# Loading A's first 1024 tokens as pairs, and issuing the first weight columns from ScalarE, in a two-headed attention and state-space kernel

## The chip, the cores and the metric

The kernel runs on one core of one Trainium2 chip. The metric is the time of one execution in device microseconds. A profiled execution also has a span, from its first to its last instruction, which leaves out what lies around it.

## What is computed

Two independent heads read two inputs of 2048 tokens by 448 and write the two halves of one output of 2048 by 896, all in bfloat16.

```python
qkv = (x @ wqkv)                      # A: 16 heads of 28, window of 8, dilation 2
idx = pos[:, None] - off[None, :]     # off = 0, 2, ..., 14
logits = einsum("bhsd,bhswd->bhsw", q, k[idx]) * 28 ** -0.5   # masked where idx < 0
a = einsum("bhsw,bhswd->bhsd", softmax(logits), v[idx]) @ wo
Bu = x2 @ B_bar.T                     # B: diagonal complex state-space model
h[t] = Lam_bar * h[t - 1] + Bu[t]
b = 2 * (h @ C.T).real + x2 * Dskip
out = concatenate([a, b], -1)
```

## The kernel before, in words

**Loads.** SP issues nearly all loads (lines 137 to 171), in the order in which they are written. The weights `wq` of A have 448 rows: three pieces of 128 rows and one of 64. `qk_load` (132) loads a range of the q and of the k columns with one DMA each for the 128-row pieces (134), and a third for the 64 rows (135). It is called for the first 128 columns and then for the other 320. POOL copies the 64 rows to partitions 64 to 127 (214 and 215), since the two halves of a pair of half-row products read them from there. A DMA that is the ninth in a row waits for the first of those before it, as there are eight semaphores for loads. ScalarE issues three small loads (`raw`, 127), the parameters of B.

**Tokens of A.** Tokens 0 to 1023 are loaded with 896-byte packets, one token each: partition p of block t holds token 128 t + p. TensorE transposes them (`XI` 273 for tokens 0 to 511, `XA` 302 and `XH` 317 for 512 to 1023), and `xi`, `xa` and `xh` copy the result into `xT`, channels on partitions and tokens along the row. Tokens 1024 to 2047 are transposed by DMA (164).

**Products of A.** `QS` (342) and `QK` (334) make q and k, 128 channels by 512 tokens at a time; `QK(u, m, 0)` is the full-row part of block m for half u of the tokens, and `QK(u, m, 1)` a pair of 64-row products which TensorE does side by side. `qk` (351) and `qh` (356) copy them from PSUM to `qf`, `kf`, `qh_t` and `kh`. `V_` (485) makes v, even and odd tokens apart. `P` (369) multiplies q with two shifted k at a time on VectorE, `E_` (381) sums over a head's channels on TensorE. Softmax follows (`lt`, `TR`, `sma`, `smb`, `smc`), then the band is laid out through DRAM (`AL`, `ad`, `sp`), and `AV` and `W_` give A's output.

**B.** `BT` is transposed by DMA (`BD` 650), `xt` (673) transposes B's tokens by DMA, `BU`, `BR`, `UP` and the scan (`sa`, `sb`, `sd`) make the states, `DN`, `H_`, `ha` to `kb` complete them, and `C(j, ct)` (826) with `c` (834) gives B's output, which `oc` stores.

**Order.** Nothing is scheduled by a compiler. `ORDER` (32) is one list of steps, found by a planner and written into the file; the loop at 885 executes it, and each engine works through its own instructions in that order. `@37` behind a step names the PSUM banks that it takes, a `.` at the end of a copy puts it on ScalarE, a `=` on VectorE. A step that is late holds all that is behind it on its engine.

Of the kernel before, what the change touches and what calls it, by code (L numbers as in the profile page):

```python
# [29 lines left out]


ORDER = """
WU@0 BD XI0@12 PP@3 xi00. pcopy pa xi30. pb pd_ XI1@4 xi31. xi01. xi21= pc xi20= tf3 QS00@5 ts03 QS10@6 XA10@7 pe
XH1@1 XA11@3 pf qk000. tf4 xa11. ts13 ts23 xa10= xh1= QK050@04 qk010= tf0 P000 ts04 QK021@27 QK031@51 pg QK051 qk051.
qk050. QK041@36 QK040 qk040. QK030 QK020 P040 ts14 ts24 qk031. QS11@4 V_011@03 qk020= QK061@12 P001 rb0 qk021. qk030.
V_111@75 qk041. QK060 ts00 qh000. qh011. V_010 v010. v011. tf5 qk011. P041 P021 tz V_110 v111. qh001. V_100@60 P020
qh010. ts10 QS01@3 qk001. V_001@45 V_101 ts20 rb1 ts05 E_00@1 E_02 ts15 v110. hc0 E_04 V_000 v001. QK100@23 v100. tf1
ts01 QK161@75 v000. P010 P011 ts11 QK101 qk101. v101. P060 QK160 P030 qh101. qk100. qh100. QK130@64 qh110. QK110@30
xt1 P050 E_01@2 QK111 qh111. P051 QK131 ts21 P031 qk110. P061 E_03 E_05 ts25 pk E_06 xt0 P100 QK141@75 xt2 qk111. P111
lt00 lt01 qk131. qk130. QK121@30 QK120 P110 hc1 qk120. xt3 qk121. tf2 V_410@12 V_411 v410= v411. QK151@46 V_511@30  # L40
V_510 v510. v511. QK150 TR0@2 P120 qk150. QK140 qk141. qk140. P101 P130 V_500@13 E_10@0 P121 qk151. ts02 tf6 E_12
V_401@45 LC V_501 v500. v501. tr0= ts06 V_400 P131 E_11@7 E_13 v400. sma0 BU201@62 P151 P150 v401. XR smb0 BU301@13
BU401@45 BU300 P140 BU400 OZ z30. BR31 BU200 z40. BU000@14 P161 z31. ci0. ci2. CD2 E_15 ts12 P141 ci3. z20. P160 E_14
E_16 lt11 lt10 ci1. CD0 CD3 BU001 z00. BU311@36 tx BU310 TR1@7 BR21 BR01 BR41 tr1. BR32 z41. z32. CD1 smc0 AL0@0 z01.
al0. ad0 OP BU210@17 xd0 BR33 z33. sma1 z21. smb1 BU010@53 BU011 xd2 ca6 BU211 BU101@40 BU100 rb2 rb3 BR02 z10. z02.
BR22 z22. ca3 cs6 BU500@24 BR11 smc1 BU501 BU111@51 BU110 pm0 z11. cs3 pm3 BR12 z12. BR23 BR03 z03= AL1@0 al1= z50.
UP3 wo BR13 AL2@5 z23. sp0 UP2 y3. BR51 UP0 z13. UP1 xd3 y2. y1. BU410@20 BU411 z51. ad1 y0= pm4 sa0 al2. BU611@67 ad2
BU601@13 BU511@45 ca4 BR42 sb0 sd0 ts22 BU600 pm2 BU510 z42. z60. BR52 z52. BR43 BR61 pm1 sa2 z43. AL3@2 al3. DN1@1
dn1 BR53 z61. z53. BU610 cs4 DN0@4 dn0 UP4 UP5 BR62 H_21@2 y4= h21 ca1 cs1 H_11@3 y5. H_20@1 sp1 sb2 z62. sd2 AV030@4
ts16 AV011@0 h20 AV010@5 av010. AV001@2 av001. av011. AV000@6 ad3 AV020@5 av000. AV031@2 sp2 av031. xd1 AV021@0 av021.  # L50
H_10@6 BR63 sp3 av020. W_31@2 h11 DN2@0 z63. W_01@1 h10 dn2 av030. W_21@5 w31. W_10@4 ow31 ca2 W_11@2 sa4 H_12@3
W_30@6 UP6 w10. w21. ca0 h12 w30. ow30 H_22@0 w11. ow11 H_01@4 DN3@5 y6. W_20@3 w20. AV131@6 av131. ts26 ow21 AV130@2
av130. ow10 AV101@7 av101. w01. AV100@3 av100. sb4 ow20 ow01 AV120@6 AV110@2 av120. AV121@7 sd4 cs2 sa6 dn3 sb6 sd6
AV111@1 av110. av121. W_70@3 w70. H_00@5 h00 W_50@6 DN4@2 h01 dn4 DN6@7 dn6 av111. DN5@3 dn5 ha24 sw6 W_40@5 ca5
H_02@1 w40. h02 W_71@4 w71. cs0 H_03@2 h03 ow40 cs5 W_61@7 H_13@3 ha16 ow71 ha25 hb16 ow70 W_60@5 ka06 sw4 hb24 W_00@4
h22 W_51@1 ha15 C33@2 w60. w00. c33 W_41@5 C31@4 ow60 sw5 w50. w61. ha14 hb15 w41. h13 C30@6 w51. C32@7 hb14 oc33 c32
oc32 H_23@5 ha26 hb26 h23 hb25 C12@0 ow41 C11@1 kb06 ow51 ka05 kb05 C10@2 ow00 ka04 C20@3 c20 c10 oc10 C22@7 C23@5
C13@3 c30 oc30 oc20 c11 C21@2 ow61 c22 oc22 c12 kb04 oc11 C01@6 c23 ow50 oc23 oc12 c21 C02@1 c01 oc01 c31 oc21 c02 c13
C00@7 c00 oc02 oc31 C03@0 c03 oc00 oc13 oc03
"""  # L60

@with_exitstack
def kernel(
# [49 lines left out]
    def evict(e, o, i):  # L113
        (ACT.copy if e == "A" else V.tensor_copy)(o, i)  # L114
# [8 lines left out]
    wq_r = A_wqkv[0:384].rearrange("(f p) n -> p f n", p=128)

    raw = const.tile([G, 3, 2, 64], BF16, tag="raw")
    for i, vec in enumerate((B_Lambda_re, B_Lambda_im, B_log_dt)):
        ACT.dma_start(raw[:, i], vec.rearrange("(g p) -> g p", p=64).unsqueeze(1).to_broadcast((G, 2, 64)))

    qk_s = wq[:, :, 0:2 * D].rearrange("p k (a n) -> p k a n", a=2)
    qk_d = A_wqkv[:, 0:2 * D].rearrange("f (a n) -> f a n", a=2)  # L130

    def qk_load(c, n):
        for a in range(2):
            SP.dma_start(qk_s[:, 0:3, a, c:c + n], qk_d[0:384, a, c:c + n].rearrange("(f p) n -> p f n", p=128))
        SP.dma_start(qk_s[0:64, 3, :, c:c + n], qk_d[384:448, :, c:c + n])

    SP.dma_start(xnA[:, 0:2], xA_r[:, 0:2])
# [2 lines left out]
    SP.dma_start(xnA[:, 4:8], xA_r[:, 4:8])  # L140
# [88 lines left out]
    pp = {}  # L229
    ops = {}  # L230

    def part(key, k, pairs, more=(False, False)):

        first = key not in begun
        begun.add(key)
        for i, pair in enumerate(pairs):
            for s, (o, l, r) in enumerate(pair):
                PE.matmul(o, l, r, start=(first and i == 0), stop=(not first and i == len(pairs) - 1 and not more[s]))  # L238
# [103 lines left out]
    def QS(m, s):  # L342
# [4 lines left out]
            PE.matmul(p[:], wqk(m, slice(0, 128), kt), xT[:, 0, 4 * s + kt], start=(kt == 0), stop=False)  # L347
        PE.matmul(p[:], wqk(m, slice(64 * s, 64 * s + 64), 3), xT[64 * s:64 * s + 64, 0, 3], start=False, stop=True)
# [571 lines left out]
```

## Time and profile before

| | us |
|---|---|
| median of 3 runs (131.54 to 132.09) | 131.96 |
| the profiled execution | 131.33 |
| its span | 129.6 |
| busy: TensorE, VectorE, ScalarE, GpSimd | 123.3, 119.6, 90.1, 21.9 |

Lines are those of the kernel's file. PE is TensorE's matmuls and PEld its weight loads, DVE is VectorE, ACT ScalarE, POOL GpSimd, SP the engine that issues DMAs; SPq and ACTq are DMA instructions in the queues of SP and ScalarE. A timeline row gives the start, the duration, the engine, the line, the operation, what it writes and reads, how many were merged into the row, and in brackets the idle time before it with what ended it. In the table of groups stand the count, the busy time, the mean of one in ns, and the idle time before them.

### The profile page before, as it was taken

The page shows a single profiled execution, that of the slowest core. Times are in us where ns is not written, and L with a number is a line of the kernel's source. Part 1 is how long each engine was busy: PE and PEld are TensorE (multiplying, and loading weights), DVE is VectorE, ACT ScalarE, POOL GpSimd, SP SyncE. Part 2 cuts the span into 40 slices and gives each one's busy share as a digit, 9 for nine tenths or more (in the row PEclk, how much of TensorE's full clock was granted, in tenths as well). Part 3 has the DMA queues.
Part 4 walks back from the last instruction along what each step waited for, and adds up shares of the span by engine and source line. Part 5 has one row for each costly group of instructions (what it writes and reads, how often), then busy time and mean ns, then how long its engine had stood idle before and what let it go on. Part 6 is the DMA issues. An engine that isn't in the chain of part 4 may idle for free. (4 is left out here: it accounts for less than half of the span.)

```text
span 129.6 us, 2872 instructions
## 1 busy us (share of the span) xinstructions
PE 123.3 (95%) x1071; PEld 61.9 (48%) x1071; DVE 119.6 (92%) x214; ACT 90.1 (70%) x182; POOL 21.9 (17%) x45
## 2 busy tenths in 40 slices
PE   6799999999999999999999999999999999999980
PEld 6643435344234434435336354955865555455530
DVE  5698999999999999999999999999999999999770
ACT  3769769999896588999997999899989440000000
POOL 6815200000000000055999200000000000000000
PEclk9999999999999999999999999999999999999999
DMA  3899997999999978575639899977330441303652
GB/s 104 198 311 284 310 202 151 236 229 229 176 229 179 222 188 342 221 139 109 221 111 193 315 237 241 202 137 118 129 94 0 150 116 38 121 21 108 210 177 71
DMA packets 44836, 22.90 MB, mean 177 GB/s; under 512 B 31063, under 2 KB 43799, under 8 KB 44823
## 3 DMA queue, kind: packets, MB, share of 16 engines
q1 hardware_dynamic: 44760, 22.72, 73.4%
q8 instruction: 8, 0.13, 0.5%
q14 instruction: 5, 0.04, 0.1%
q10 hardware_dynamic: 63, 0.01, 0.0%
HBM read 11.56 MB, written 6.29 MB: 138 GB/s over the span
## 5 line engine op out<-in xcount | busy, mean ns | idle before, releaser
L378 DVE TENSOR_TENSOR pr<-qf,kf 128x2048 bf16<-128x2048 bf16 x24 | 28.1, 1216 | 0.0
L238 PE MATMUL ps<-xbuf,BT 128*128 128x512 bf16 (+1 forms) x112 | 23.4, 379 | 0.0
L831 PE MATMUL ps<-Cw,Z 128*128 128x448 bf16 x112 | 21.7, 353 | 0.0
L238 PE MATMUL ps<-xT,wq 128*128 128x512 bf16 (+1 forms) x96 | 20.8, 380 | 0.2
L831 PEld LDWEIGHTS <-Z 128*128 128x128 bf16 x112 | 10.9, 98 | 10.4 <-DVE Z L800 0.3
L114 ACT CAST Z<-ps 128x512 bf16<-128x512 f32 (+1 forms) x32 | 14.8, 525 | 1.3 <-PE ps L701 0.8
L238 PEld LDWEIGHTS <-BT 128*128 128x128 bf16 (+1 forms) x112 | 8.8, 97 | 12.7 <-issue 3.4
L524 PE MATMUL ps<-wo,oT 128*128 128x448 bf16 x64 | 14.0, 353 | 0.2 <-ACT oT L114 0.2
L238 PE MATMUL ps<-wq,xT 128*128 128x448 bf16 (+1 forms) x64 | 13.1, 353 | 0.0
L238 PEld LDWEIGHTS <-wq 128*128 128x128 bf16 (+1 forms) x96 | 7.5, 97 | 11.1 <-issue 3.8
L877 POOL MEMSET PT<- 128x4320 f32 x3 | 11.0, 3703 | 8.6 <-PE ps L394 8.6
L114 ACT CAST ya<-ps 128x448 bf16<-128x448 f32 (+1 forms) x17 | 8.8, 546 | 3.8 <-PE ps L524 1.6
L837 DVE TENSOR_TENSOR xbuf<-ps,xnB 128x448 bf16<-128x448 f32 x16 | 9.2, 616 | 1.5 <-PE ps L831 1.5
L114 ACT CAST oT<-ps 128x512 bf16<-128x512 f32 x17 | 9.2, 620 | 0.5 <-PE ps L511 0.5
L663 ACT ACTIVATE ctmp<-Cw,c2t 64x448 f32<-64x448 bf16 x14 | 9.3, 666 | 0.2
L524 PEld LDWEIGHTS <-oT 128*128 128x128 bf16 x64 | 6.2, 98 | 6.2 <-ACT oT L114 0.7
L114 ACT CAST v_s<-ps 128x448 bf16<-128x448 f32 x15 | 7.5, 534 | 1.8 <-PE ps L238 1.8
L511 PE MATMUL ps<-PT,v_s 128*32 128x135 bf16 (+1 forms) x256 | 8.4, 299 | 0.0
L238 PEld LDWEIGHTS <-xT 128*128 128x128 bf16 (+1 forms) x64 | 5.2, 97 | 6.6 <-issue 2.4
L772 DVE TENSOR_TENSOR Z<-ps,Z 128x512 bf16<-128x512 f32 x12 | 8.0, 682 | 0.0
L114 ACT CAST qf<-ps 128x512 bf16<-128x512 f32 x11 | 6.2, 585 | 2.5 <-PE ps L238 2.4
L511 PEld LDWEIGHTS <-v_s 128*32 128x32 bf16 x256 | 7.0, 111 | 0.5 <-issue 0.5
(161 smaller groups left out, 195.1 us busy)
## 6 DMA issues: line engine op xcount, KB each, us to landing
PT<-pd SPq DMA_DIRECT2D x16, 156.0 KB, 3.8
xnB<-in_B_x_dram SPq DMA_DIRECT2D x2, 896.0 KB
out_dram<-ya SPq DMA_DIRECT2D x16, 112.0 KB, 3.6
out_dram<-xbuf SPq DMA_DIRECT2D x16, 112.0 KB, 1.7
pd<-Ak SPq DMA_DIRECT2D x2, 640.0 KB, 5.3
xbuf<-in_A_x_dram SPq DMA_DIRECT2D x2, 448.0 KB
xnB<-in_B_x_dram SPq DMA_DIRECT2D x4, 224.0 KB, 5.9
xnB<-in_B_x_dram SPq DMA_DIRECT2D x4, 192.0 KB, 4.7
```

Source lines behind the costliest of these rows:

```text
L114: (ACT.copy if e == "A" else V.tensor_copy)(o, i)
L238: PE.matmul(o, l, r, start=(first and i == 0), stop=(not first and i == len(pairs) - 1 and not more[s]))
L378: V.tensor_tensor(t[:], q.unsqueeze(1).to_broadcast((128, 4, 512)), k4, ALU.mult)
L511: PE.matmul(p[32 * hh:32 * hh + 32, 128 * bl:128 * bl + n], v_s[:, t, 4 * hg + hh, :], PT[:, t % NS, (4 * hg + hh) // HS, (4 * hg + hh) % ...
L524: PE.matmul(p[:, 0:D], late["oT"][:, b // 4, hg, par, 128 * (b % 4):128 * (b % 4) + 128], late["wo"][:, hg, :], start=(hg == 0), stop=(hg ...
L663: ACT.activation(t[a:a + 64, 0:D], Cw[b:b + 64, g, :], ACTF.Copy, scale=c2t[a:a + 64, g:g + 1])
L772: V.tensor_tensor(zz, pp.pop(("h", j, g))[:], zz, ALU.add)
L831: PE.matmul(p[:, 0:D], z, Cw[:, g, :], start=(g == 0), stop=(g == G - 1))
L837: V.tensor_tensor(yo, pp.pop(("c", j, ct))[:, 0:D], xnB[:, ct, j, :], ALU.add)
L877: POOL.memset(late["PT"][:, 4 * i:4 * i + 4].rearrange("p t g n -> p (t g n)").bitcast(F32), 0.0)
```

## The change

A's tokens 0 to 1023 are loaded as pairs: partition p of a block of 256 tokens holds tokens 2p and 2p + 1, which lie side by side in DRAM, 1792 bytes. So the transposed row of a block has its 128 even tokens first and its 128 odd tokens behind them. The copies of q and k of this half read PSUM with a step of 128 elements, so that their output is in the order of the tokens again. `V_` takes the even and the odd tokens of this half as they now lie. The first 128 columns of q and k are issued by ScalarE (the two DMAs of 128-row pieces; the 64 rows stay on SP), and `raw` by SP behind them. `ORDER` is written anew throughout; the steps are the same ones. 19 copies change between ScalarE and VectorE.

```diff
+    def qk_load(c, n, q):
+        for a in range(2):
+            q.dma_start(qk_s[:, 0:3, a, c:c + n], qk_d[0:384, a, c:c + n].rearrange("(f p) n -> p f n", p=128))
+        SP.dma_start(qk_s[0:64, 3, :, c:c + n], qk_d[384:448, :, c:c + n])
+
+    xb = xbuf.rearrange("p (b n) -> p b n", n=2 * D)
+    xb_r = A_x[0].rearrange("(b p i) d -> p b (i d)", p=128, i=2)
+    SP.dma_start(xb[:, 0], xb_r[:, 0])
+    SP.dma_start(xb[:, 1], xb_r[:, 1])
+    qk_load(0, 128, ACT)
     raw = const.tile([G, 3, 2, 64], BF16, tag="raw")
     for i, vec in enumerate((B_Lambda_re, B_Lambda_im, B_log_dt)):
-        ACT.dma_start(raw[:, i], vec.rearrange("(g p) -> g p", p=64).unsqueeze(1).to_broadcast((G, 2, 64)))
...
-    SP.dma_start(xnA[:, 0:2], xA_r[:, 0:2])
-    SP.dma_start(xnA[:, 2:4], xA_r[:, 2:4])
-    qk_load(0, 128)
-    SP.dma_start(xnA[:, 4:8], xA_r[:, 4:8])
-    qk_load(128, 320)
+        SP.dma_start(raw[:, i], vec.rearrange("(g p) -> g p", p=64).unsqueeze(1).to_broadcast((G, 2, 64)))
+    SP.dma_start(xb[:, 2:4], xb_r[:, 2:4])
+    qk_load(128, 320, SP)
...
+    def qk_copy(u, o, i, e):
+
+        if u == 0:
+            o = o.rearrange("p (h n i) -> p h n i", h=2, i=2)
+            i = i.rearrange("p (h i n) -> p h n i", h=2, i=2)
+        evict(e, o, i)
...
-        evict(e, kf[:, f, HALO + tok:HALO + tok + 512] if m % 2 else qf[:, f, tok:tok + 512], pp["qk", u, m][s][:])
+        qk_copy(u, kf[:, f, HALO + tok:HALO + tok + 512] if m % 2 else qf[:, f, tok:tok + 512], pp["qk", u, m][s][:], e)
...
-        evict(e, kh[r, u, HALO:] if a else qh_t[r, u, :], pp["qk", u, 6][s][64 * a:64 * a + 64, :])
+        qk_copy(u, kh[r, u, HALO:] if a else qh_t[r, u, :], pp["qk", u, 6][s][64 * a:64 * a + 64, :], e)
...
+        c = slice(c + par, c + 256, 2) if b0 >= 4 else slice(c + 128 * par, c + 128 * par + 128)
```

The first lines of `ORDER`, before and after, and the first line of the last third after it:

```diff
-WU@0 BD XI0@12 PP@3 xi00. pcopy pa xi30. pb pd_ XI1@4 xi31. xi01. xi21= pc xi20= tf3 QS00@5 ts03 QS10@6 XA10@7 pe
-XH1@1 XA11@3 pf qk000. tf4 xa11. ts13 ts23 xa10= xh1= QK050@04 qk010= tf0 P000 ts04 QK021@27 QK031@51 pg QK051 qk051.
-qk050. QK041@36 QK040 qk040. QK030 QK020 P040 ts14 ts24 qk031. QS11@4 V_011@03 qk020= QK061@12 P001 rb0 qk021. qk030.
+WU@0 XI0@12 xi20. xi00= XI1@3 xi01. xi30= PP@4 pcopy pa xi31. xi21= pb pe QS10@5 pc qk010. XH1@6 XA10@7 xa10. XA11@1
+xa11. QS00@0 qk000. xh1= QK021@24 QK031@35 pd_ QK041@67 tf3 QK050@10 QK030 pf qk031. qk030. tf5 P000 ts05 ts03 tz pg
+QK040 qk040. xt0 BD QK020 qk021. qk041. rb3 ts13 P001 rb0 qk020. ts23 QS01@5 QK051 qk001. QK061@36 V_111@47 qk050. rb1
...
+ha26 C11@6 oc30 w50. ow50 H_03@1 c10 hb25 oc10 hb26 ow41 h03 ka06 C32@3 c11 ka04 ka05 kb05 kb04 h00 C23@5 w51. ow51
+kb06 oc11 C12@0 c12 c23 c32 C22@1 c22 oc32 C20@6 C21@2 c21 oc22 C00@0 c13 oc12 oc23 C03@5 c00 oc00 c03 c20 oc13 oc21
```

More of the change, by code (lines that the diff above doesn't have):

```diff
@@ L32 @@
 ORDER = """
-WU@0 BD XI0@12 PP@3 xi00. pcopy pa xi30. pb pd_ XI1@4 xi31. xi01. xi21= pc xi20= tf3 QS00@5 ts03 QS10@6 XA10@7 pe
-XH1@1 XA11@3 pf qk000. tf4 xa11. ts13 ts23 xa10= xh1= QK050@04 qk010= tf0 P000 ts04 QK021@27 QK031@51 pg QK051 qk051.
-qk050. QK041@36 QK040 qk040. QK030 QK020 P040 ts14 ts24 qk031. QS11@4 V_011@03 qk020= QK061@12 P001 rb0 qk021. qk030.
-V_111@75 qk041. QK060 ts00 qh000. qh011. V_010 v010. v011. tf5 qk011. P041 P021 tz V_110 v111. qh001. V_100@60 P020
-qh010. ts10 QS01@3 qk001. V_001@45 V_101 ts20 rb1 ts05 E_00@1 E_02 ts15 v110. hc0 E_04 V_000 v001. QK100@23 v100. tf1
@@ L38 @@
[L38 to L57, printed above, removed]
@@ L58 @@
-C13@3 c30 oc30 oc20 c11 C21@2 ow61 c22 oc22 c12 kb04 oc11 C01@6 c23 ow50 oc23 oc12 c21 C02@1 c01 oc01 c31 oc21 c02 c13
-C00@7 c00 oc02 oc31 C03@0 c03 oc00 oc13 oc03
+WU@0 XI0@12 xi20. xi00= XI1@3 xi01. xi30= PP@4 pcopy pa xi31. xi21= pb pe QS10@5 pc qk010. XH1@6 XA10@7 xa10. XA11@1
+xa11. QS00@0 qk000. xh1= QK021@24 QK031@35 pd_ QK041@67 tf3 QK050@10 QK030 pf qk031. qk030. tf5 P000 ts05 ts03 tz pg
+QK040 qk040. xt0 BD QK020 qk021. qk041. rb3 ts13 P001 rb0 qk020. ts23 QS01@5 QK051 qk001. QK061@36 V_111@47 qk050. rb1
@@ new lines @@
+V_110 qk051. ts15 v110. QK060 tf4 ts04 P041 qh010. V_100@25 P040 QS11@1 qh011. ts25 V_101 v101. v100. V_011@04 V_010
+v010. QK100@65 E_00@2 qh001. P020 P021 E_02 qk011. P050 ts14 E_04 QK101 V_001@01 qh000. v011. v111. QK161@34 qk100.
+qk101. hc0 P030 QK160 qh101. P051 qh110. P011 hc1 V_000 QK110@76 xt1 v001. ts24 P010 P031 tf1 P061 E_01@5 E_03 qh111.
+v000. rb2 qh100. xt2 E_05 QK121@14 QK141@03 QK111 P060 qk110. P100 QK140 xt3 ts01 P101 qk141. LC QK120 qk111. P110
+qk121. E_06 qk140. qk120. lt00 lt01 QK130@73 QK131 qk131. V_401@64 XR tf0 ts11 QK151@01 V_511@25 V_510 qk130. P121
@@ new lines @@
+v510. P120 v511. TR0@3 tr0. V_400 v400. QK150 sma0 P111 v401. V_500@72 V_410@53 V_411 pk V_501 ts00 ts10 ts21 OZ
+qk151. qk150. E_10@6 E_12 E_11@4 ts20 P141 v410. v501. v411= v500. BU401@10 smb0 BU301@52 ci3. P150 BU201@37 BU200
+BU300 ci1. z30. BU400 BR31 z20. BR21 P131 ci0. P151 P140 E_14 CD3 z31. P130 E_13 P160 E_15 CD1 z40. z21. BR41 z41.
+ci2. P161 CD2 smc0 BU000@53 E_16 lt11 CD0 BU001 z00= lt10 tf6 BU101@21 BU311@70 BU310 TR1@4 BR32 tr1. AL0@6 BR01 BU100
+al0. ad0 OP sma1 BU210@54 pm0 z10. z01. BR11 smb1 z11. xd1 BU010@62 BU011 BU211 BU111@31 pm3 z32. smc1 BR33 ca6 tf2 wo
@@ new lines @@
+sp0 pm2 BR02 z02. z33. BU110 BR12 z12. BR22 AL2@7 BR03 BR13 pm4 z22. AL1@6 cs6 z13= UP3 xd3 z03. UP0 al2. al1. y0.
+AL3@3 UP1 y1= sa0 y3. BR23 BU500@57 BU501 ca3 ca1 BU511@62 BU601@01 BU600 ad1 al3= z60. z50. z23= xd2 ts02 UP2 y2.
+BU510 sb0 sd0 cs3 ad2 BR51 BR61 BU410@30 BU411 pm1 BU611@54 ts06 BR42 z51. z61. z42. sp1 BR52 DN0@7 z52. ts12 ts22
+BU610 BR43 BR53 DN1@1 cs1 z43. BR62 sa2 AV030@3 z53. av030. dn0 AV020@6 av020. AV001@7 av001. AV000@3 av000. AV021@6
+av021. AV011@7 av011. AV031@3 AV010@6 UP4 H_20@7 sb2 z62. UP5 dn1 av010. ad3 sd2 DN2@1 y4. av031. xd0 BR63 h20 DN3@5
@@ new lines @@
+dn3 ts16 z63. H_10@6 ca0 W_01@0 y5= W_21@3 ts26 W_30@7 sp2 dn2 H_02@5 w21. UP6 sp3 w30. W_31@2 y6. sa4 cs0 w01. W_10@1
+w31. w10. W_11@3 H_11@7 H_12@4 h02 W_20@0 ow31 H_01@2 sb4 ow21 h10 ca4 w11. h11 sd4 AV101@5 av101. AV130@1 ow10 ca5
+av130. AV131@6 sa6 AV100@3 h12 ow30 cs4 sb6 AV110@7 h01 av100. AV111@5 av111. AV120@1 ow01 av131. AV121@3 av121. DN4@5
+H_21@4 dn4 w20. ow20 sw4 W_61@6 H_23@3 ow11 av110. h23 av120. ca2 w61. sd6 W_51@0 DN5@2 dn5 W_70@7 w70. H_22@5 h22
+W_50@1 H_13@3 W_71@2 ha15 tx h13 cs2 W_40@6 ow70 DN6@7 dn6 ow61 W_00@5 sw5 cs5 h21 C30@3 C33@7 w71. sw6 ha25 ha16 ha24
@@ L60 @@
+w40. c33 W_41@2 w41. oc33 ow71 ha14 w00. hb15 ow00 hb14 hb16 C31@6 c31 oc31 W_60@4 c30 C13@7 ow40 hb24 H_00@2 C10@5
+ha26 C11@6 oc30 w50. ow50 H_03@1 c10 hb25 oc10 hb26 ow41 h03 ka06 C32@3 c11 ka04 ka05 kb05 kb04 h00 C23@5 w51. ow51
+kb06 oc11 C12@0 c12 c23 c32 C22@1 c22 oc32 C20@6 C21@2 c21 oc22 C00@0 c13 oc12 oc23 C03@5 c00 oc00 c03 c20 oc13 oc21
+C01@3 c01 C02@1 w60. ow60 oc20 c02 oc01 oc03 oc02
 """
@@ L123 @@
     wq_r = A_wqkv[0:384].rearrange("(f p) n -> p f n", p=128)
+    qk_s = wq[:, :, 0:2 * D].rearrange("p k (a n) -> p k a n", a=2)
+    qk_d = A_wqkv[:, 0:2 * D].rearrange("f (a n) -> f a n", a=2)
+    def qk_load(c, n, q):
[7 more added lines that the diff above has]
+    qk_load(0, 128, ACT)
     raw = const.tile([G, 3, 2, 64], BF16, tag="raw")
     for i, vec in enumerate((B_Lambda_re, B_Lambda_im, B_log_dt)):
[L127 to L137, printed above, removed]
-    SP.dma_start(xnA[:, 2:4], xA_r[:, 2:4])
-    qk_load(0, 128)
-    SP.dma_start(xnA[:, 4:8], xA_r[:, 4:8])
-    qk_load(128, 320)
+        SP.dma_start(raw[:, i], vec.rearrange("(g p) -> g p", p=64).unsqueeze(1).to_broadcast((G, 2, 64)))
+    SP.dma_start(xb[:, 2:4], xb_r[:, 2:4])
+    qk_load(128, 320, SP)
     SP.dma_start(wq[:, 0:3, 2 * D:], wq_r[:, :, 2 * D:])
@@ L487, in V_ @@
         c = 256 * (b0 % 2)
+        c = slice(c + par, c + 256, 2) if b0 >= 4 else slice(c + 128 * par, c + 128 * par + 128)
         part(("v", b0, par), k,
-             [[(p[s][:, 0:D], xT[64 * s:64 * s + 64, b0 // 4, 3, c + par:c + 256:2], wq[64 * s:64 * s + 64, 3, 2 * D:3 * D])
+             [[(p[s][:, 0:D], xT[64 * s:64 * s + 64, b0 // 4, 3, c], wq[64 * s:64 * s + 64, 3, 2 * D:3 * D])
                for s in range(2)]] if k else
-             [[(p[s][:, 0:D], xT[:, b0 // 4, 4 * s + kt, c + par:c + 256:2], wq[:, kt, 2 * D:3 * D])
+             [[(p[s][:, 0:D], xT[:, b0 // 4, 4 * s + kt, c], wq[:, kt, 2 * D:3 * D])
                for s in range(2)] for kt in range(3)])
```

## The prediction

> **What bounds the kernel now.** I read the page first, then busy time by stages, then the waits of PE, then the first 13 us instruction by instruction.
>
> ```profile
> span 129.6 us, 2872 instructions
> ...
> PE 123.3 (95%) x1071; PEld 61.9 (48%) x1071; DVE 119.6 (92%) x214; ACT 90.1 (70%) x182; POOL 21.9 (17%) x45
> ...
> PE   6799999999999999999999999999999999999980
> ```
>
> ```profile
> 0.00:6.39 6.39, 4.45 (x53) 4.21 (x53) 3.85 (x11) 3.48 (x9) 4.92 (x29) 1.00 0.62 148
> 6.39:12.55 6.16, 5.96 (x39) 2.29 (x38) 5.51 (x19) 5.06 (x16) 2.04 (x5) 1.00 1.14 303
> 12.55:56.34 43.79, 43.68 (x325) 17.77 (x323) 43.10 (x65) 36.85 (x73) 0.92 (x5) 1.00 1.00 220
> 56.34:126.01 69.67, 69.22 (x668) 37.65 (x660) 66.71 (x122) 44.73 (x87) 14.05 (x6) 1.00 0.58 145
> 126.01:129.60 3.59, 0.00 (x0) 0.00 (x0) 0.41 (x1) 0.00 (x0) 0.00 (x0) 1.00 0.29 93
> ```
>
> The columns of the second view are the stretch, its length, then PE, PEld, DVE, ACT, POOL, the granted clock, the DMA share and GB/s. From 12.55 to 126.01 PE is idle for 0.11 + 0.45 = 0.56 us of 113.46, at a granted clock of 1.00, and VectorE for 3.65 us. So the body is bound by TensorE, with VectorE close behind it, and the last 3.59 us are the way of the last output. A change that removes no matmul can gain in three places only: before 12.55 us, in what the order of the matmuls itself costs, and in the few short waits of the body. The start, instruction by instruction:
>
> ```profile
> 0.80 0.59 ACTq L127 DMA_DIRECT2D raw<-in_B_Lambda_re_dram  x1
> ...
> 0.81 0.45 SPq L137 DMA_DIRECT2D xbuf<-in_A_x_dram  x1
> ...
> 1.82 1.04 SPq L134 DMA_DIRECT2D wq<-in_A_wqkv_dram  x2
> ...
> 2.91 0.74 SPq L135 DMA_DIRECT2D wq<-in_A_wqkv_dram  x1
> ...
> 3.70 0.58 SPq L140 DMA_DIRECT2D xbuf<-in_A_x_dram  x1
> ...
> 3.82 0.61 PE L285 MATMUL ps<-ident,xbuf 128*128 128x128 bf16 x8
> ...
> 4.36 0.59 ACT L114 CAST xT<-ps 128x512 bf16<-128x512 f32 x1 [0.76 <-PE ps L285]
> ...
> 4.36 0.25 PE L549 MATMUL ps<-ident,raw 7*128 7x7 bf16 x3
> ...
> 5.40 0.61 SPq L135 DMA_DIRECT2D wq<-in_A_wqkv_dram  x1
> ...
> 6.39 1.03 PE L347 MATMUL ps<-xT,wq 128*128 128x512 bf16 x3 [0.89 <-ACT xT L114]
> ...
> 10.04 0.61 POOL L215 COPY wq<-wq 64x512 bf16<-64x512 bf16 x1 [3.20 <-DMA wq<-in_A_wqkv_dram]
> ...
> 11.57 0.55 PEld L238 LDWEIGHTS <-wq 64*128 64x128 bf16 x8 [0.56 <-issue]
> ...
> 12.54 1.41 PEld L238 LDWEIGHTS <-wq 128*128 128x128 bf16 x8 [0.42 <-issue]
> ```
>
> The first real product (L347) begins at 6.39 and waited for ScalarE's copies of the transposed tokens, not for a load. At 12.54 PE has done two QS blocks, 16 transposes of tokens 512 to 1023, QK050 and four half-row pairs (QK021, QK031, QK051, QK041). I measure the start by this point. POOL's copy of the last 64 weight rows (L215) did wait for a load, until 10.04. How the loads go:
>
> ```profile
> GB/s 0 0 0 0 0 0 0 6 107 155 204 354 367 349 348 278 175 132 137 160 127 110 87 147 143 253 362 372 330 352 348 348 348 361 358 333 257 211 238 257
> ...
> xbuf<-in_A_x_dram SPq DMA_DIRECT2D x2, 224.0 KB, 3.0
> ...
> wq<-in_A_wqkv_dram SPq DMA_DIRECT2D x2, 96.0 KB, 3.1
> ...
> wq<-in_A_wqkv_dram SPq DMA_DIRECT2D x1, 80.0 KB, 4.6
> ```
>
> Each figure of the first row is a slice of 0.24 us of the first 9.5. The 896-byte packets of x reach 350 GB/s after a slow rise (slices 9 to 11, and again 22 to 25). The 256-byte packets of the first weight columns, alone from slice 16 to 22, move 110 to 175.
>
> **The change part by part.** *Loads.* ScalarE issues the two DMAs that took SP 1.04 us (L134). The three small raw loads go the other way, at up to 0.59 each (the first on ScalarE). SP therefore reaches the next x load at about 3.7 or a little later, and nothing is gained in issue. The gain is overlap: the 0.2 MB of first columns (two times 96 KB and 32 KB) no longer follow x0 and x1 but run beside them. At 130 to 175 GB/s they took slices 16 to 22, some 1.6 us; at 350 they would take 0.7. That is up to 0.9 us off the stream. Packets twice as long can shorten only the two slow rises, about 0.4 us each; at 350 GB/s there is nothing left to win. No row shows a 1792-byte packet. Bounds for the last 64 rows (80 KB, landing at 5.40 + 4.6 = 10.0): not earlier, or earlier by 0.9 + 0.8 = 1.7. I take 0.85, half of it, since the rises return at the same place (slice 22) whatever stood in front of them.
>
> [...]
>
> *The new start of the order.* QS10, the transposes, QS00, then three half-row pairs, then QK050. VectorE now takes xi00 beside ScalarE's xi20, so the copies end sooner. The half-row pairs need POOL's copy: 10.0 - 0.85 = 9.15, then 0.04 and 0.61, 9.8. PE is ready before: x0 landed near 0.81 + 3.0 = 3.8; the weights beside it add and the longer packets take off. With the copies shared by two engines QS10 begins by 6.2 and ends by 7.2. The transposes need the next x load. It is 448 KB, issued at about 3.7, and the row's next fast rise (slices 25 to 28) puts its end near 7 now, so 6.2 to 7.2 after. They take about 0.9, QS00 1.1: 8.4 to 9.3.
>
> ```profile
> 7.35 0.39 PE L348 MATMUL ps<-xT,wq 64*128 64x512 bf16 x1
> 7.67 0.82 PE L347 MATMUL ps<-xT,wq 128*128 128x512 bf16 x3
> 8.43 0.39 PE L348 MATMUL ps<-xT,wq 64*128 64x512 bf16 x1
> ```
>
> The three matmuls of L347 from 7.67 end 0.82 later, the last one taking 0.38, so one starts every 0.22 us. To the next row form it is more: from 7.35 to 7.67 is 0.32, and from 7.67 to 8.43 is 0.76 where 3 x 0.22 would be 0.66. **A change between matmuls of 128 and 64 rows costs PE 0.10 us.** So from 9.8: 3 x 0.22, 0.10 and 6 x 0.22 make 2.08, to 11.88. QK051 is left over, 0.22: 12.1 against 12.54. That is **-0.44** (bounds 0 and -1.2: the landing as it was makes 12.95 of it, and then the wait is the rival below; the fastest loads find PE not ready before 8.4 to 9.3).
>
> *Changes of form.* I counted the places in both orders where the PE tile changes (128 rows, 64 rows, 32 columns, and the 7-row transposes): 43 before, 39 after. Eight and six of them lie ahead of the point at 12.54 and are in the term above. Two are left: **-0.2**.
>
> *The strided copies.* All 16 copies of q and k for the first 1024 tokens now read PSUM with a step of 512 bytes and stand on ScalarE; two of them were VectorE's.
>
> ```profile
> L114 ACT CAST kf<-ps 128x512 bf16<-128x512 f32 x11 | 6.3, 593 | 0.5 <-PE ps L238 0.3
> ...
> L114 ACT COPY attn<-ps 128x1024 bf16<-128x1024 bf16 x1 | 1.0, 1023 | 0.0
> ...
> L114 DVE CAST kf<-ps 128x512 bf16<-128x512 f32 x1 | 0.7, 692 | 0.0
> ...
> L114 DVE COPY xT<-ps 128x1024 bf16<-128x1024 bf16 x1 | 0.7, 681 | 0.0
> ```
>
> No row shows a stepped read. Below zero is excluded: as many elements are read and written. The upper end is the time of twice the elements, 1023 - 593 = 0.43 each, 6.9 us in all. I take **0**, by the nearest rows: ScalarE's copies of one length cost the same whatever is behind them, 0.84 ns an element (0.43 for 512 more). [...]
>
> *Moves between engines.* VectorE gives up xa10 (0.68) and two q copies, and takes xi00 and a few others: about 0.9 us less, ScalarE some 1.7 more. ScalarE idles 43.79 - 36.85 = 6.9 us between 12.55 and 56.34, which hides it: 0. The cover is thin before 33 us:
>
> ```profile
> 13.00:33.00 20.00, 19.89 (x120) 8.28 (x118) 19.55 (x37) 17.32 (x39) 0.81 (x4) 1.00 1.12 228
> ```
>
> There it is 2.7 us. If it were gone, PE would wait for PSUM banks, one for one.
>
> *raw behind x on SP* (two loads of 0.45, one of 0.74) is issued 1.6 us later, so the transposes of raw go from 4.36 to 6.0 at worst. pcopy and pa stand ahead of xi21 and xi31 in their queues, and QS10 waits for those: it ends by 7.7 then, still ahead of the wait until 9.8. 0, at worst +0.3. *V_* reads its tokens side by side instead of every other one: 0, since loading weights of xT took as long as those of wq.
>
> ```profile
> L238 PEld LDWEIGHTS <-xT 128*128 128x128 bf16 x48 | 4.5, 98 | 5.2 <-issue 1.3
> L238 PEld LDWEIGHTS <-wq 128*128 128x128 bf16 x72 | 6.6, 98 | 9.0 <-issue 2.1
> ```
>
> *Exp's table* (tx) is loaded behind the last sine instead of between, one load more on ScalarE at about 100 us, where it idles (25 us from 56.34): 0. *BD* goes behind one B transpose on SP, ten us ahead of its reader: 0. *The end* is again C, its sum and one output: 0. The body's 0.56 us of waits I leave as they are.
>
> Sum: -0.44 - 0.2 = -0.64. The profiled execution took 131.33, 1.73 more than its span; by it the changed kernel has a span of 129.0 and a time of 130.7. The median of the runs is 0.63 above that execution: 131.96 - 0.64 = **131.3**.
>
> **The rivals.** *First, the loads come faster still* (both rises and the narrow columns gone, 1.2 us at PE): 131.96 - 1.2 - 0.2 = 130.6. For it: 256-byte packets are visibly the slow stretch. Against: the second rise has nothing to do with them.
>
> *Second, the loads land no earlier*: the change doesn't do what it says. The half-row pairs then wait until 10.65 and the point comes at 12.95, 0.4 late; less 0.2 for the forms, 132.1. For it: x already moves at 350 GB/s. [...]
>
> *Third, slower: the stepped read costs ScalarE time.* Place: 13 to 33 us. 16 x 0.43 = 6.9 us, of which the idle 2.7 hide a part: 4.2, so 135.5. It decides from a price of 2.7 / 16 = 0.17 us a copy. For it: no row shows such a read. [...] Against: ScalarE's time goes by elements in every row.
>
> *Fourth, the body's new order waits.* VectorE idles only 3.65 us of the body, and a product of L378 that comes late holds the E_ matmul behind it:
>
> ```profile
> L378 DVE TENSOR_TENSOR pr<-qf,kf 128x2048 bf16<-128x2048 bf16 x24 | 28.1, 1216 | 0.0
> ```
>
> One such and one copy late by their whole length (1.22 + 0.59) take 1.8: 133.1. For it: in the last third C(2,1) and C(0,0) take PSUM banks that VectorE frees just ahead of them (h00, c12). Against: VectorE has 0.9 us less to do.
>
> **How the numbers follow.** Forecast 0.35 (131.3, own range 130.9 to 131.8); loads faster 0.15 (130.6); loads no earlier 0.15 (132.1); stepped read 0.17 (135.5); new waits 0.18 (133.1). 0.5% is 0.66 us, about what a measurement here can tell from no change: faster is below 131.3, slower above 132.6. Faster: a little over half of the forecast, 0.2, the first rival's 0.15, and 0.02: 0.37. Slower: 0.17, 0.17 of the new waits and 0.02: 0.36. Same: the rest, 0.27. The range goes from 130.3 to 134.2; it leaves out most of the stepped read's case and a little below.
>
> **What would show it.** The copies of q and k on ScalarE with a mean near 593 (right) or near 1020 (third rival). POOL's L215 copy starting near 9.2 rather than 10.04. PE's first L347 near 6 and QK030 near 11.9. PE idle in the body near 0.6 us. Wrong would be ScalarE named as releaser of PE before 33 us, or VectorE after 66.

## The result, and the profile after

The changed kernel takes 136.29 us (median of 4 executions, 135.13 to 137.76) against 131.90 of the kernel before, measured beside it: 1.030 times as long, 95% interval 1.027 to 1.034. The ratio leaves out the execution of 137.76 us, which is counted as a slow one. The prediction said 131.3 and a range up to 134.2. The sign was wrong, and the time lies above the range.

The profiled execution took 135.13, 3.80 more than that of before. Its page, with the lines that answer to those shown of before:

```profile
span 133.4 us, 2869 instructions
...
PE 124.4 (93%) x1071; PEld 63.4 (48%) x1071; DVE 123.0 (92%) x213; ACT 92.8 (70%) x184; POOL 22.4 (17%) x45
...
PE   6989999999999999999981999999999999999990
```

(A MEMSET of GpSimd's writes zeros and reads nothing; it is called a fill below.) Two things stand out. VectorE is busy 3.4 us longer (123.0 against 119.6) although the same steps are computed and some copies have left it for ScalarE. And one slice of PE (the 22nd, 70.0 to 73.4 us) has a 1, where no slice of the body was below 9. The same stretches as before, cut at the same times:

```profile
12.55:56.34 43.79, 43.77 (x313) 18.27 (x310) 42.79 (x62) 40.09 (x83) 1.00 (x5) 1.00 1.09 226
56.34:126.01 69.67, 66.12 (x657) 35.88 (x656) 67.98 (x122) 45.30 (x87) 14.05 (x6) 1.00 0.50 128
126.01:133.40 7.39, 3.93 (x21) 1.84 (x19) 3.38 (x6) 0.00 (x0) 0.00 (x0) 0.97 0.55 175
```

Until 56.34 PE is idle for 0.02 us, so the body up to there is as full as before. From there to 126.01 it is idle for 3.55 us, where it was 0.45. The waits of PE name who it waited for (total, times, longest):

```profile
PE ps L722 <- DVE Z L114: 3.1, 2, 2.9
...
PE ps L348 <- DVE xT L114: 0.6, 1, 0.6
PE ps L466 <- DVE attn L447: 0.4, 1, 0.4
PE ps L239 <- POOL wq L216: 0.3, 1, 0.3
```

The large one is `UP` (722), waiting for a copy of z on VectorE. Read back along VectorE's queue, in the timeline of the changed kernel, the copy is not slow but late:

```profile
57.40 3.70 POOL L886 MEMSET PT<- 128x4320 f32 x1 [10.16 <-PE ps L402]
57.58 0.95 DVE L446 RECIPROCAL z<-z 128x128 f32<-128x128 f32 x1
...
60.31 0.94 DVE L629 TENSOR_SCALAR kM<-iot,fT 128x256 int32<-128x256 f32 x1
...
68.01 3.70 POOL L886 MEMSET PT<- 128x4320 f32 x1
68.23 3.62 DVE L629 TENSOR_SCALAR kM<-iot,fT 128x256 int32<-128x256 f32 x1
...
71.89 0.48 DVE L630 SCALAR_TENSOR_TENSOR fr<-iot,fT,kM 128x256 f32<-128x256 f32 x1
72.29 0.68 DVE L676 SCALAR_TENSOR_TENSOR Cw<-Cw,c1t,ctmp 128x448 bf16<-128x448 bf16 x1
72.89 0.42 DVE L114 CAST Z<-ps 128x256 bf16<-128x256 f32 x1
...
73.36 0.27 PE L722 MATMUL ps<-Z,R 128*128 128x256 bf16 x1 [2.90 <-DVE Z L114]
```

One instruction of 256 numbers a partition, `kM` in the step `tf2` (the `tf` steps make the phases for B's sine tables), takes 3.62 us. It starts 0.22 behind GpSimd's fill of `PT` and ends at 71.85, 0.14 behind that fill's end (68.01 + 3.70 = 71.71). The one at 60.31 (`tf6`) ends at 61.25, 0.15 behind the end of the first fill (61.10). Not every VectorE instruction with one input is held: the RECIPROCAL at 57.58 ends at 58.53, inside the same fill, and takes 0.95 us. Behind the long one, in VectorE's order, stand `fr`, a step of C, and the copy for which `UP` waits. What the instruction costs when no fill runs is in the row of its line (least, median, most, in ns), first after, then before:

```profile
L629 DVE TENSOR_SCALAR kM<-iot,fT x7: 346/353/3619, 10.1 to 68.2; 128x256 int32<-128x256 f32 x7
```

```profile
L620 DVE TENSOR_SCALAR kM<-iot,fT x7: 343/344/347, 6.9 to 44.3; 128x256 int32<-128x256 f32 x7
```

Before, the last `kM` ran at 44.3, and GpSimd's first fill of `PT` began at 56.55:

```profile
56.55 3.70 POOL L877 MEMSET PT<- 128x4320 f32 x1 [8.60 <-PE ps L394]
...
64.77 7.34 POOL L877 MEMSET PT<- 128x4320 f32 x2
```

So the two never met before. The new order put `tf6` behind `lt10` and `tf2` behind `ca6`, among the fills `pm0` to `pm4`. The extra time, (3.62 - 0.35) + (0.94 - 0.35) = 3.86 us, is more than VectorE's whole growth of 3.4. That it is a hold by the fill was a reading of starts and ends so far; the experiments tested it.

### The profile page after: what moved, and what is told of

Its sections match the earlier page's. It is cut to its first block, busy times and chain, and to the rows that moved or that the text cites. A ratio compares the mean times of both kernels' runs of the same rounds, so it can differ in the third digit from the quotient of the medians.

```text
span 133.4 us, 2869 instructions
## 1 busy us (share of the span) xinstructions
PE 124.4 (93%) x1071; PEld 63.4 (48%) x1071; DVE 123.0 (92%) x213; ACT 92.8 (70%) x184; POOL 22.4 (17%) x45
## 4 chain that ended last, share of the span: by engine, by line
PE 69%; DVE 12%; ACT 6%; issue 4%; POOL 4%; DMA 2%; POOLq 0%; DVEq 0%; ACTq 0%
PE ps L239 28%; PE ps L840 16%; PE ps L533 9%; PE ps L520 6%; DVE kM L629 3%; PE ps L398 3%; ACT Cn L114 3%; ACT Z L114 2%; DMA Cw<-Cn 2%; PE ps L776 2%; PE ps L710 1%; DVE Z L114 1%; PE ps L348 1%; DVE attn L447 1%; ACT attn L437 1%
## 5 line engine op out<-in xcount | busy, mean ns | idle before, releaser
L114 ACT CAST Z<-ps 128x512 bf16<-128x512 f32 (+1 forms) x30 | 14.2, 518 | 3.7 <-PE ps L239 3.3
L114 ACT CAST ya<-ps 128x448 bf16<-128x448 f32 x16 | 7.8, 543 | 4.2 <-issue 3.4
L114 ACT CAST kf<-ps 128x512 bf16<-128x512 f32 x12 | 6.8, 599 | 2.1 <-PE ps L239 2.0
```

## The experiments

The kernel before, measured again beside each group of runs, took 131.98 to 132.07 us; ratios are to the time measured beside the run, with 95% intervals. A difference of 0.1 or 0.2 us between two runs is within these intervals. The first theory says that a GpSimd fill holds VectorE's `kM` until it ends, and that this is the loss. Its rivals: the loss is in the start and the order anyway; any VectorE work there is held, or DMAs do it; the two share bandwidth.

**The two steps ahead of the fills.**

```diff
- ... lt10 tf6 BU101@21 ...  ca6 tf2 wo ...
- ... ts20 P141 ...
+ ... ts20 tf6 tf2 P141 ...
```

> The changed kernel with the two phase steps tf6 and tf2 moved ahead of GpSimd's fills of PT (behind ts20, at about 45 us), nothing else. Theory 1 (VectorE's kM instruction is held for as long as a GpSimd fill runs, and that is most of the loss): all seven kM take 0.35 us, PE's wait of 2.9 us at 70 us and the 0.4 us at 68 us go, and the time falls by about 3 us, to 132.5 to 133.5. Theory 2 (the loss sits in the start and in the order of the other steps, and the long kM only fills a time in which VectorE would have waited for something else): PE stands still for 2 us or more at the same place with another releaser, and the time stays above 135.

132.89 us, 1.0071 (1.0047 to 1.0095). No `kM` is long (most 0.48 us) and PE's wait at 70 us is gone: 3.4 us of the loss. But not all: PE now waits 1.22 us at 49.65 for a copy of v that VectorE does late, since `tf6` and `tf2` (1.66 us together) stand ahead of it. Where VectorE is full, the place of a step has a price even without a fill.

**The same place, another form of the instruction.**

```diff
- V.tensor_scalar(kM, iot[:], fT[:, g:g + 1], None, ALU.mult)
+ V.scalar_tensor_tensor(kM, iot[:], fT[:, g:g + 1], zt[:, 0:N2], ALU.mult, ALU.add)
```

> The changed kernel with kM made by a scalar_tensor_tensor (the same product, plus a tile of zeros) instead of a tensor_scalar, at the same places beside the fills. Theory 1, in the form that only VectorE's one-input form is held by the fill: all seven kM take about 0.48 us, and the time falls by 3.9 - 7 x 0.13 = 3 us or a little less, to 132.7 to 134. Theory 3 (any VectorE work on those tiles at that moment is held, or the DMAs of the stage do it): kM still takes some 3 us at about 68 us and the time stays at 136.

131.64 us, 0.9975 (0.9956 to 0.9995): all of the loss is gone, by one changed line. That is a us less than the 132.7 expected at the least; that sum took off the time of `kM` alone. Two stretches of its timeline and the row of the line:

```profile
10.02 0.85 POOL L216 COPY wq<-wq 64x512 bf16<-64x512 bf16 x1 [3.21 <-DMA wq<-in_A_wqkv_dram]
...
10.43 0.71 DVE L629 SCALAR_TENSOR_TENSOR kM<-iot,fT,zt 128x256 int32<-128x256 f32 x1
...
57.33 3.70 POOL L886 MEMSET PT<- 128x4320 f32 x1 [10.16 <-PE ps L402]
...
60.23 0.48 DVE L629 SCALAR_TENSOR_TENSOR kM<-iot,fT,zt 128x256 int32<-128x256 f32 x1
...
67.69 0.48 DVE L629 SCALAR_TENSOR_TENSOR kM<-iot,fT,zt 128x256 int32<-128x256 f32 x1
67.92 3.70 POOL L886 MEMSET PT<- 128x4320 f32 x1
```

```profile
L629 DVE SCALAR_TENSOR_TENSOR kM<-iot,fT,zt x7: 477/479/712, 9.4 to 67.7; 128x256 int32<-128x256 f32 x7
```

With two inputs the instruction takes 0.48 us beside the fills, at 60.23 inside one; only beside GpSimd's copy, at 10.43, which also reads, does it take 0.71. The one at 67.69 starts 0.23 ahead of its fill here, where it started 0.22 behind it in the changed kernel, so it isn't the same meeting; the next run has that. So the rows differ by form and by what GpSimd does: 3.62 for one input beside a fill of 3.70, which reads nothing, 0.48 for two inputs inside such a fill, 0.71 for two inputs beside a copy. Why the one form is held and the other not, no run here shows.

**Only the long hold taken away** (the new form for `tf2` alone).

```diff
+ if g in (2,):
+     V.scalar_tensor_tensor(kM, ...)
+ else:
      V.tensor_scalar(kM, iot[:], fT[:, g:g + 1], None, ALU.mult)
```

> The changed kernel with kM as scalar_tensor_tensor for tf2 alone (the one held for 3.62 us); tf6 keeps its tensor_scalar beside the first fill of PT (0.94 us in the changed kernel). If the long hold is nearly all of the loss: PE's wait of 2.9 us goes, the one of 0.4 us before it (L466 behind the softmax on VectorE) stays, and the time is 131.6 to 132.2. If the short hold matters as much through what it shifts: 133 or more.

131.89 us, 0.9992 (0.998 to 1.0004). The last fill and `tf2` meet as they did in the changed kernel, 0.23 us behind the fill's start, and with two inputs nothing holds it:

```profile
67.72 3.70 POOL L889 MEMSET PT<- 128x4320 f32 x1
...
67.95 0.48 DVE L630 SCALAR_TENSOR_TENSOR kM<-iot,fT,zt 128x256 int32<-128x256 f32 x1
```

The short hold is still there (0.94 us, PE waits 0.4 for the softmax); the 0.25 us to the run above (131.89 - 131.64) may be its price, but the intervals of the two overlap. So the one instruction at 68.23 made the loss.

**The fills cut up.**

```diff
- POOL.memset(late["PT"][:, 4 * i:4 * i + 4] ..., 0.0)
+ for t in range(4 * i, 4 * i + 4):
+     for g in (0, 2):
+         POOL.memset(late["PT"][:, t, g:g + 2] ..., 0.0)
```

> The changed kernel with each of GpSimd's three fills of PT (3.7 us each) cut into eight of 0.46 us; same order, same bytes. Theory 1, in the form that the fill holds VectorE until the instruction ends: kM ends with the small fill that it met, so it takes at most 0.35 + 0.46 = 0.8 us, and the time falls by 2.5 to 3 us, to 133 to 134. Theory 4 (fill and kM share the memory's bandwidth, the fill being served first as long as it has work): cutting changes nothing, kM takes 3.6 us again and the time stays at 136.

131.95 us, 1.0004 (0.9985 to 1.0023), below the 133 to 134 expected. In its timeline:

```profile
57.28 4.12 POOL L888 MEMSET PT<- 128x540 f32 x8 [10.15 <-PE ps L402]
...
60.19 0.73 DVE L629 TENSOR_SCALAR kM<-iot,fT 128x256 int32<-128x256 f32 x1
60.22 0.55 POOL L888 MEMSET PT<- 128x540 f32 x1
...
67.38 1.17 POOL L882 MEMSET ya<- 128x1280 f32 x1
...
67.91 0.79 DVE L629 TENSOR_SCALAR kM<-iot,fT 128x256 int32<-128x256 f32 x1
...
68.48 4.13 POOL L888 MEMSET PT<- 128x540 f32 x8
```

The old one-input `kM` of `tf6` slips in between two of eight fills and takes 0.73 us, in the middle of 4.12 us of filling that goes on behind it: it ends at 60.92, 0.15 behind the end of one small fill (60.77). Had it waited for as long as filling went on, it would have ended after 61.40. So the unit of the hold is GpSimd's instruction. This rests on `tf6`. The `kM` of `tf2`, which made the loss, does not meet the cut fill here: it starts at 67.91, beside the uncut fill of `ya`, and ends 0.15 behind that one, and the last filling of `PT` begins at 68.48. So a part of this run's gain is that the two no longer meet.

**The reverse: the kernel before, made to meet a fill.**

```diff
- ... ts02 tf6 E_12 ...  tr0= ts06 V_400 ...  smc1 BU501 ...
+ ... ts02 E_12 ...      tr0= V_400 ...       smc1 tf6 ts06 BU501 ...
```

> The kernel before with tf6 and ts06 alone moved back, behind smc1, where GpSimd fills PT (64.8 to 72.1 us); everything else as before. Theory 1: that one kM takes 2 to 3 us instead of 0.34, PE waits about as long shortly after 70 us, and the time rises by 1.5 to 3 us, to 133.5 to 135. Theory 2: kM costs what it costs elsewhere, and the time stays within 0.7 us of 131.9.

138.76 us, 1.0511 (1.0465 to 1.0557): slower, as theory 1 had it, but by 6.7 us and not by 1.5 to 3. Its timeline shows the hold as expected (`kM` ends at 72.61, 0.15 behind the second of the two fills) and a longer chain behind it:

```profile
65.11 7.35 POOL L877 MEMSET PT<- 128x4320 f32 x2
...
69.63 2.98 DVE L620 TENSOR_SCALAR kM<-iot,fT 128x256 int32<-128x256 f32 x1
72.64 0.48 DVE L621 SCALAR_TENSOR_TENSOR fr<-iot,fT,kM 128x256 f32<-128x256 f32 x1
...
73.16 0.51 ACT L636 ACTIVATE tab<-fr,cols 128x256 bf16<-128x256 f32 x1 [3.65 <-DVE fr L621]
73.58 0.56 ACT L114 CAST Z<-ps 128x512 bf16<-128x512 f32 x1
74.19 1.44 PE L701 MATMUL ps<-Z,R 128*128 128x512 bf16 x3 [4.85 <-ACT Z L114]
```

ScalarE's sine waited 3.65 us for `fr`, the copies of z stood behind it, and PE waited 4.85. And then PE ran slow. The stretches behind the wait (PE's busy time is the first figure behind the length, the granted clock the third from the end):

```profile
72.00:73.00 1.00, 0.00 (x0) 0.00 (x0) 0.96 (x2) 0.00 (x0) 0.46 (x1) 0.83 0.02 2
73.00:74.00 1.00, 0.00 (x0) 0.00 (x0) 0.72 (x2) 0.84 (x2) 0.00 (x0) 0.50 0.00 0
...
79.00:80.00 1.00, 1.00 (x5) 0.36 (x4) 0.80 (x3) 1.00 (x3) 0.00 (x0) 0.75 0.65 254
80.00:82.00 2.00, 2.00 (x14) 0.68 (x13) 1.85 (x5) 1.95 (x4) 0.00 (x0) 1.00 0.42 169
```

The clock falls to half at 72.66 (0.83 of the first stretch at 1.00 and 0.50: one third of it at half), 3.3 us after PE's last matmul (74.19 - 4.85 = 69.34), and is back in the middle of the stretch from 79 to 80: 6.8 us at half rate. PE was at work from 74.19 on, so by an estimate it lost another 2.7 us (half of the 5.3 to 79.5): the wait cost more than its length. This profile's mean clock is 0.975; of the other three executions one has 0.975 too and two have 0.984 and 0.985.

This is also the likely reason why the changed kernel's median stands 1.2 us above its profiled execution. Its four executions took 135.13, 136.23, 136.35 and 137.76 us at mean granted clocks of 0.998, 0.986, 0.987 and 0.975. By an estimate from the 3.4 us at half the clock that the run with `raw` back on ScalarE shows below, one such stretch is 1.7 of 134.5, 0.0127: it would make 0.987. A PE wait of 2.9 us seems to set it off in most executions, though not in the profiled one; the profile of such an execution was not taken, so this is argued and not shown.

**The loads alone, and the order alone.** The kernel before with the pairs, the loads and the stepped copies but its own `ORDER`; and the kernel before with the new `ORDER` and the two-input `kM`.

```diff
  loads and copies: the changed kernel's
- ORDER = the new one
+ ORDER = the one before
```

> The kernel before with its own order, but with the pairs, the loads from ScalarE, raw on SP and the stepped copies. Theory A: 131.6 (0.44 under 132.07). Theory B: 132.1 within 0.2. Theory C: 132.3 or more, since in this order the transposes of raw (PP) stand ahead of everything but XI0, and raw now lands some 2 us later: PE's first L348 then begins after 7 us.

```diff
  loads and copies: the kernel's before
- ORDER = the one before
+ ORDER = the new one
- V.tensor_scalar(kM, ...)
+ V.scalar_tensor_tensor(kM, ...)
```

> The new order (with kM as scalar_tensor_tensor, so that the fills hold nothing) with the loads, the layout of the tokens and the copies of the kernel before. Beside the run with everything new and that kM (131.64), it shows what the loads and the pairs are worth within the new order. Theory A (the load term of the prediction, -0.44, holds): without them about 132.1. Theory B (the loads land no earlier, the second rival): the same 131.6 within 0.2. Theory C (the new loads cost something, as GpSimd's copy of the 64 rows began 0.2 us later than before): 131.3 or less.

The loads in the old order: 133.81 us, 1.0143 (1.0087 to 1.0199). There PP stands ahead of `XI1`, `raw` is late, and PE's first L348 begins at 7.70 (6.39 before). Its executions lie in two groups, 132.7 to 133.1 and 134.6 to 134.9; why was not settled (two of the upper three show a granted clock of 1.00, so it is not the clock in them). This is theory C. The order without the loads: 131.61, 0.998 (0.9964 to 0.9995). With everything new and the same `kM` it was 131.64. So in the new order the pairs, the second issuer and the stepped copies are worth nothing that these runs can tell, in either direction, and what is gained, some 0.4 us, goes with the order and the two-input `kM`; the kernel before with that `kM` alone was not run.

**The 64 rows first**, with the new loads, and with the old ones in the new order. Both have the two-input `kM`.

```diff
 def qk_load(c, n, q):
+    SP.dma_start(qk_s[0:64, 3, :, c:c + n], ...)
     for a in range(2):
         q.dma_start(qk_s[:, 0:3, a, c:c + n], ...)
-    SP.dma_start(qk_s[0:64, 3, :, c:c + n], ...)
```

> The changed kernel with kM as scalar_tensor_tensor, and in each part of the q and k columns the 64 rows issued ahead of the 128-row pieces. The 80 KB that GpSimd's second copy waits for then stand one place further ahead on SP, by 1.0 us of issue. Expected if the place in the queue decides: the copy begins near 9.0 instead of 10.0 and the half-row pairs some 0.7 us earlier; time 131.0 to 131.3. If the bytes ahead decide (all land together at the end of a full stream): copy at 9.8 to 10.0 and 131.6.

> The new order with the loads and token layout of before (131.61) and the 64 rows first. Theory B (pairs and ScalarE's issue are worth nothing): as the new loads with the 64 rows first, 131.4 within 0.2. Theory A (they are worth up to 0.44 once the 64 rows are out of the way): 131.6 or more, with PE waiting for the first weight columns and for x as in the run without this edit (0.8 and 0.7 us).

131.40 us with the new loads, 0.996 (0.994 to 0.9979); 131.30 with the old ones, 0.9941 (0.992 to 0.9962). Again the loads make no difference clear of the intervals; both beat the kernel before, and the second has the lowest median of this study. The timelines of the changed kernel and of the run with the new loads and the 64 rows first:

```profile
5.55 0.62 SPq L131 DMA_DIRECT2D wq<-in_A_wqkv_dram  x1
...
10.24 0.71 POOL L216 COPY wq<-wq 64x512 bf16<-64x512 bf16 x1 [3.39 <-DMA wq<-in_A_wqkv_dram]
```

```profile
4.53 0.62 SPq L129 DMA_DIRECT2D wq<-in_A_wqkv_dram  x1
...
8.52 0.63 POOL L216 COPY wq<-wq 64x512 bf16<-64x512 bf16 x1 [1.72 <-DMA wq<-in_A_wqkv_dram]
```

Issued 1.02 us earlier, the 80 KB are there 1.72 earlier. The other profiles agree: GpSimd's copy begins between 9.88 and 10.70 in all nine with the 64 rows last, and between 8.44 and 8.76 in the four with them first (the run with `raw` on ScalarE, below, apart). So what stands ahead of them in SP's queue sets when they land; they do not all land together at the end of one stream. PE no longer waits for them.

**Two attempts to mend the start**, both with the 64 rows first and the new `kM` for `tf6` and `tf2` alone: PP, `pcopy` and `pa` behind `QS10`; then `pc` and `pe` behind `xh1` as well.

```diff
- xi30= PP@4 pcopy pa xi31. xi21= pb pe QS10@5 pc qk010. ... qk000. xh1= QK021@24
+ xi30= xi31. xi21= QS10@5 PP@4 pcopy pa pb pe qk010. pc ... qk000. xh1= QK021@24
+ xi30= xi31. xi21= QS10@5 PP@4 pcopy pa qk010. pb ... qk000. xh1= pc pe QK021@24
```

> A version meant to gain: the changed kernel with the 64 rows first, kM as scalar_tensor_tensor for tf6 and tf2 alone, and PP, pcopy and pa behind xi31, xi21 and QS10. Expected: the first L348 begins near 6 and isn't interrupted (0.6 us of PE's wait goes), the half-row pairs as in the run with the 64 rows first; 130.6 to 131.2 if both hold, 131.6 if the landing of the weights bounds the start anyway.

> As the earlier attempt to mend the start (131.74, where VectorE's eight small steps of pe stood ahead of the copy xh1 and PE waited 0.8 us for it), but with pe and pc behind xh1. Expected: PE runs from the first L348 to the half-row pairs with no wait over 0.3 us, and the time is 130.7 to 131.2. If it stays at 131.4 or more, VectorE is late for the first products of q and k instead.

131.74 us (0.998, 0.9964 to 0.9996) and 131.56 (0.9957, 0.994 to 0.9974). In the first, PE waited 0.8 us for `xh1` behind the steps of `pe`; in the second, PE's waits behind 5 us are 0.3 us or less each and nothing is gained over 131.40. So the stall in the first product (0.63 us in the changed kernel) was covered, as the prediction had said; what it delays seems to wait for loads or for VectorE's products later in any case.

**`raw` back on ScalarE** (with the 64 rows first and the two-input `kM`).

```diff
-        SP.dma_start(raw[:, i], ...)
+        ACT.dma_start(raw[:, i], ...)
```

> The run with the 64 rows first (131.40), and raw issued by ScalarE behind the first columns instead of by SP. SP reaches the second x load 1.5 us earlier. If issue bounds the landing: that load and what is behind it land up to 1 us earlier, the transposes of raw earlier too, 130.6 to 131.1. If the bytes bound it: raw's transposes earlier (PE's wait of 0.7 us in the first product gets shorter), the rest as it was, 131.2 to 131.5. ScalarE's first copy may come later, behind its table load: then 131.5 to 131.9.

133.27 us, 1.0065 (1.0037 to 1.0092): slower than every theory had it. The 64 rows, issued at 3.62, are there at 7.35, as the place in the queue says. But `raw` comes later from ScalarE than from SP, and PE waits 1.17 us for it and 0.90 for a copy behind it. Then:

```profile
6.00:8.00 2.00, 0.50 (x2) 0.30 (x4) 0.61 (x2) 1.09 (x4) 1.36 (x3) 1.00 0.99 241
8.00:9.00 1.00, 0.57 (x2) 0.05 (x1) 0.88 (x7) 0.57 (x6) 0.00 (x0) 0.61 0.90 288
9.00:10.00 1.00, 1.00 (x8) 0.56 (x8) 0.64 (x4) 0.43 (x2) 0.00 (x0) 0.50 0.95 293
...
11.50:12.00 0.50, 0.50 (x3) 0.12 (x1) 0.46 (x2) 0.50 (x2) 0.00 (x0) 0.86 1.01 252
12.00:13.00 1.00, 1.00 (x9) 0.31 (x7) 0.93 (x3) 0.91 (x2) 0.00 (x0) 1.00 1.11 317
```

From about 8.2 to 11.6 the clock is at half. No single wait was longer than 1.2 us; PE was busy for 0.50 of the 2.00 us ahead of it, and for 1.57 of the 3.40 us ahead of 8.20. The executions of this run show what that costs: four at a mean granted clock of 0.996 to 1.000 took 131.79 to 132.41 us, seven at 0.986 or 0.987 took 133.12 to 133.61, and one at 0.974 took 134.12. So most of what this run lost is the clock.

## Why the prediction was wrong, point by point

- **The body's waits "I leave as they are": this step failed.** They rose from 0.56 us to 3.57, nearly all of it one wait of 2.90 behind one instruction, and a clock that falls behind the wait seems to add 1.2 us to the median. The prediction compared the lengths of the steps, the engines on which they stand and the loads. It never asked which GpSimd instruction runs beside which VectorE instruction. That they would meet could have been seen: `tf2` and `tf6` moved from 38 and 44 us into the stretch in which the trace of before shows GpSimd's fills. What no row of before could show was the hold and its length, since no `kM` met a fill there.
- **The fourth rival** had the right engine (VectorE late, 133.1) with the wrong place and price: it looked at the last third and at steps of their usual length. From 66 us on VectorE named as releaser was the sign that it gave, and that is what came.
- **Loads, -0.44: wrong, it is 0** (131.61 against 131.64, 131.30 against 131.40). GpSimd's copy began at 10.24, not 9.2: between 9.88 and 10.33 in six profiles with the new loads, between 10.04 and 10.70 in three with the old ones. The overlap with the first columns is there, but what stands ahead of the 64 rows in SP's queue sets their landing. The point at which the prediction measured the start came late, too: the weights of QK050 begin at 11.74, and 6 x 0.22 and 0.22 more make it 13.3, where 12.1 was forecast and 12.54 stood before. With the two-input `kM` it is 13.2 by the same sum (weights from 11.66), and the time is still 0.4 below that of before. So what the order gains, it gains behind that point; where was not traced. The second rival was right that the loads land no earlier (10.24 against 10.04 before). Its time, 132.1, was not reached, because the order gained beside it.
- **Changes of form, -0.2.** The order without the hold, with the two-input `kM`, is worth some 0.4 us in all (131.61 against 131.98, 131.64 against 132.07). How much of it is the forms was not measured by itself.
- **Strided copies, 0: right.** Half of the copies in each of these rows of the changed kernel are stepped; before the change the means were 593 and 585 (of `kf` and `qf`). The third rival falls: it needed 0.17 us a copy, and the means, with half of the copies stepped, rose by 6 ns.

```profile
L114 ACT CAST kf<-ps 128x512 bf16<-128x512 f32 x12 | 6.8, 599 | 2.1 <-PE ps L239 2.0
L114 ACT CAST qf<-ps 128x512 bf16<-128x512 f32 x12 | 6.7, 591 | 0.8 <-PE ps L239 0.6
```

- **`raw` on SP, 0, at worst +0.3: right for this order, for the reason given** (the wait until about 10 covers it; mending it gained nothing). QS10 ended at 8.6 rather than 7.7, so the size of the delay was too small. In the old order the same move, with the other new loads, costs 1.8 us.
- **Moves between engines, `V_`, BD, the end: 0.** Not measured one by one. The new order without the hold is no slower than the old one, so they cannot cost much together, and PE waits for no ScalarE copy between 12.55 and 33 us in the changed kernel.

## What to carry to other kernels

When an order is written anew, lay the GpSimd instructions beside the VectorE ones in time, and look for a VectorE instruction like `kM`, a `tensor_scalar` with its one input and its output in SBUF, that falls into a long GpSimd instruction: here it ended 0.14 to 0.15 us behind the other's end, each time. (The RECIPROCAL, one input too, was not held: 0.95 us, ended inside a fill.) Three cures were measured here: keep the two apart in time, use a two-input form (0.48 us instead of 0.35, not held by any fill here), or cut the fill (eight of 0.55 us instead of one of 3.70). A long wait of PE is to be priced at more than its length: behind one of 4.85 us the clock stood at half for 6.8 us, another 2.7 us by the estimate above. For the one of 2.90 us this is argued and not shown.
